# Loading the SwiGLU input weights first and multiplying them on VectorE, in a one-token attention and MLP kernel

## The chip, the cores and the metric

The kernel runs on one core of a Trainium2 chip. The metric is the device time of one execution in microseconds (us), the median of several executions. TensorE appears as PE (matmuls) and PEld (weight loads), VectorE as DVE, ScalarE as ACT, GpSimd as POOL and SyncE as SP.

## What is computed

One token `x` of 512 numbers is layer-normalised to `xn`, and two branches are added to it, all in float32:

```python
xn  = layernorm(x)
# attention over a cache: 32 heads, 4096 positions, 128 numbers a head
q   = (xn @ wq).reshape(32, 128)                       # wq 512 x 4096
s   = einsum("hd,hkd->hk", q, k_cache) * 128 ** -0.5   # k_cache 32 x 4096 x 128
o   = einsum("hk,hkd->hd", softmax(s), v_cache)
A   = o.reshape(4096) @ wo                             # wo 4096 x 512
# a gated MLP on the same token, weighted by its router score
g   = silu(xn @ w_gate); u = xn @ w_up                 # both 512 x 1376
y   = ((g * u) @ w_down) * sigmoid(xn @ w_r)           # w_down 1376 x 512
out = x + A + xn + y
```

With one token chosen out of one, the selection and the scatter of the original reference do nothing. The inputs are 159.45 MB, nearly all of it `k_cache` and `v_cache` (67.1 MB each), `wq` and `wo` (8.4 MB each) and the three MLP matrices (2.8 MB each).

## The kernel before

SBUF holds three large slots of 64 KB per partition: S0, S1 and S2. All large loads are issued by SP, in program order, one after another in one queue. Each goes to 128 partitions, except that `wo` is cut into seven pieces of 8, 8, 6, 5, 3, 1 and 1 rows per partition (`PIECES`).

The order of the queue is `wq` into S0; `k_cache` of groups 0 and 1 into S1 and S2; and then for each group g of four heads the values V[g] into S0 and the keys K[g+2] into the slot that group g's keys had. V[7] goes to S1. After the loop come `w_gate` and `w_up` (L76, both into S0), `w_down` (L246, into S2) and the pieces of `wo` (L251, into S1). A load into a slot waits, on SP, until the slot's earlier contents have been read, and everything behind it in SP's program waits with it.

The work runs in this order. VectorE normalises `x` and TensorE spreads it to `xb` (L163, L166), one column per partition. TensorE makes all queries in `ps_q` (L173), as soon as `wq` is there. For each group `scores(g)` multiplies the keys by the query on VectorE in place (L206), adds them up (L207), takes a maximum (L208 to L211), and ScalarE exponentiates (L214). `values(g)` multiplies probabilities and values on TensorE (L225, 32 matmuls of 512 columns, each issued as two instructions since it is float32), and gathers the head's own rows from the result (L230, L232).

After the loop TensorE turns the attention output into columns (`ot`, L273, L275); multiplies gate and up (`ffn_in`, L280), the 1376 hidden units lying along the free axis, 344 in each of four partition groups; VectorE and ScalarE make `hid`, and VectorE spreads it over partitions (four copies at L299, a transpose at L304, a masking at L306) to suit `w_down`, which was loaded as a flat run of 5504 numbers per partition; TensorE multiplies `w_down` in 43 matmuls (L312); ScalarE copies `y` (L315). Last, `add` (L324) sums everything into four accumulators of 128 columns: the residual first, then `y`, then 32 rows of `wo`, each as four matmuls. TensorE runs its instructions in program order, so no row of `wo` is multiplied before `y` is ready. Two copies on ScalarE and two on VectorE (L338, L340) and two stores (L341, L342) end the kernel.

Of the kernel before, what the change touches and what calls it, by code (L numbers as in the profile page):

```python
# [23 lines left out]
def kernel(  # L24
# [13 lines left out]
    nc = tc.nc  # L38
    _, H, Sk, Dh = k_cache.shape
    D = x.shape[-1]  # L40
    F = w_gate.shape[1]
    NK = D // P
    C = Sk // PP
    NG = H // HP
    DC = D // NCOL
    FC = F // NCOL
    FW = F * D // P
    NQ = FW // DC
    FA = F // PP
# [8 lines left out]
    def sb(name, shape, dt=F32):  # L58
        return const.tile(shape, dt, name=name)

    pad = sb("pad", [P, 96])
    S0, S1, S2 = (sb(f"slot{i}", [P, SLOT]) for i in range(3))


    KS = [S1, S2] * (NG // 2)
    VS = [S0] * (NG - 1) + [S1]

    loads = []

# [12 lines left out]
    x_row, xn = (t[0:1].rearrange("o c h -> o (c h)") for t in PT)  # L82
    xc = pv[0:1].rearrange("o c d -> o (c d)")
    loads.append(nc.scalar.dma_start(x_row, x[0]))
    wr_row = sb("wr_row", [1, D])
    loads.append(nc.scalar.dma_start(wr_row, w_r.rearrange("(o n) -> o n", o=1)))
    WQ = load_rows(wq, S0).rearrange("p (j g h d) -> p j g h d", j=NK, h=HP, d=Dh)
    K, V = {g: load_cache(k_cache, g, KS[g]) for g in range(2)}, {}


    ps_q = [psum.tile([P, 512], F32, name=f"ps_q{i}") for i in range(2)]
    ps_pv = [psum.tile([P, 512], F32, name=f"ps_pv{i}") for i in range(2)]
    ps_o = psum.tile([P, 512], F32, name="ps_o")
    ps_acc = psum.tile([P, 512], F32, name="ps_acc")
    ps_a = psum.tile([P, 512], F32, name="ps_a")
    ps_b = psum.tile([P, 512], F32, name="ps_b")
    for t in (ps_a, ps_b, ps_acc, *ps_pv):
        nc.vector.memset(t, 0.0)

    ones = sb("ones", [1, P])  # L100
    nc.vector.memset(ones, 1.0)
    eps_t = sb("eps_t", [1, 1])
    nc.vector.memset(eps_t, EPS)

    WIN = 2 * H - HP

    ints = sb("ints", [P, NQ * NCOL], I32)  # L110

    def hits(n, pattern, base, mult, mask):
        it = ints[:n]
        for _, k in pattern[::-1][:-1]:
            it = it.rearrange("p (a b) -> p a b", b=k)
        if len(pattern) == 1:
            it = it[:, :pattern[0][1]]
        else:
            it = it[:, :pattern[0][1], :]
        nc.gpsimd.iota(it, pattern=pattern, base=base, channel_multiplier=mult)  # L120
        if mask:
            nc.vector.tensor_scalar(it, it, mask, None, op0=ALU.bitwise_and)
        return it
# [3 lines left out]
    it = hits(P, [[-HP, G], [-1, HP]], 0, 1, 31)  # L127
# [6 lines left out]

    ew = sb("ew", [H, P + HP - 1])
    it = hits(H, [[1, P + HP - 1]], 1 - HP, -HP, 0)
    nc.vector.tensor_scalar(ew, it, 0, None, op0=ALU.is_equal)

    sy = sb("sy", [P, NCOL, PP])
    nc.gpsimd.memset(sy, 0.0)  # L140
    it = hits(P, [[-1, NCOL]], 0, 1, 31)
    nc.vector.tensor_scalar(sy[:, :, 0], it, 0, None, op0=ALU.is_equal)

    own = sb("own", [P, NQ, NCOL])
    it = hits(P, [[1, NQ], [-1, NCOL]], 0, 3, 3)
    nc.vector.tensor_scalar(own, it, 0, None, op0=ALU.is_equal)


    s1 = sb("s1", [1, 1])
    nc.vector.reduce_sum(s1, x_row, axis=AX.X)  # L150
    mean = sb("mean", [1, 1])
    nc.vector.tensor_scalar(mean, s1, 1.0 / D, None, op0=ALU.mult)
    nc.vector.tensor_scalar(xc, x_row, mean, None, op0=ALU.subtract)
    nc.vector.tensor_tensor(xn, xc, xc, op=ALU.mult)
    s2 = sb("s2", [1, 1])
    nc.vector.reduce_sum(s2, xn, axis=AX.X)
    std = sb("std", [1, 1])
    nc.scalar.activation(std, s2, AF.Sqrt, bias=eps_t, scale=1.0 / D)
    rstd = sb("rstd", [1, 1])
    nc.vector.reciprocal(rstd, std)  # L160
    nc.vector.tensor_scalar(xn, xc, rstd, None, op0=ALU.mult)  # L161
    for j in range(NK):
# [15 lines left out]
    nc.vector.tensor_tensor(wr_row, wr_row, xn, op=ALU.mult)  # L178
    r = sb("r", [1, 1])
    nc.vector.reduce_sum(r, wr_row, axis=AX.X)  # L180
    nc.tensor.matmul(ps_b[:, 0:1], ones, r, start=True, stop=True)  # L181
    base = wr_row
    nc.vector.tensor_tensor(base, x_row, xn, op=ALU.add)

    for t in PT:
        last_pool = nc.gpsimd.memset(t, 0.0)

    def sigmoid(z, e):
        nc.scalar.activation(e, z, AF.Exp, scale=-1.0)  # L189
        nc.vector.tensor_scalar(e, e, 1.0, None, op0=ALU.add)  # L190
        nc.vector.reciprocal(e, e)
        return e

    sr = sigmoid(ps_b[:, 0:1], sb("sr", [P, 1]))

    sc = [sb(f"sc{i}", [P, C]) for i in range(2)]
    rs = sb("rs", [P, NG])
    m = sb("m", [P, 1])
# [36 lines left out]
    for g in range(NG):  # L235
        scores(g)
        V[g] = load_cache(v_cache, g, VS[g])
        if g + 2 < NG:
            K[g + 2] = load_cache(k_cache, g + 2, KS[g + 2])
        values(g)  # L240


    W_GATE = load_rows(w_gate, S0[:, :FW]).rearrange("p (j f) -> p j f", f=F)
    W_UP = load_rows(w_up, S0[:, FW:2 * FW]).rearrange("p (j f) -> p j f", f=F)
    WD = S2[:, :FW].rearrange("p (j n) -> p j n", n=DC)
    loads.append(nc.sync.dma_start(S2[:, :FW], w_down.rearrange("f n -> (f n)").rearrange("(p j) -> p j", p=P)))  # L246
    WO = S1.rearrange("p (r n) -> p r n", n=D)
    src = wo.rearrange("(p r) n -> p r n", p=P)
    a = 0
# [6 lines left out]
    for i in (*loads, last_pool):  # L256
        tc.add_manual_dep(seen.ins, i.ins.name, mybir.DependencyInfo(mybir.DependencyClass.Sync, mybir.DependencyReason.DATA),
                          reason="seen before the store")
    at = [FW]

    def spare(n):
        at[0] += n
        return S2[:, at[0] - n:at[0]]

    rinv = sb("rinv", [H, 1])
# [4 lines left out]
    for c in range(HP):  # L272
        nc.tensor.matmul(ps_pv[0][:, :R], ew[:, HP - 1 - c:HP - 1 - c + P], o_n[:, c * R:(c + 1) * R],  # L273
                         start=(c == 0), stop=(c == HP - 1))
    nc.vector.tensor_copy(ot, ps_pv[0][:, :R])  # L275

    def ffn_in(W, ps):
        for j in range(NK):
            for t in range(NCOL):
                nc.tensor.matmul(ps[PP * t:PP * t + 1, :FC], xb[:, j, 0:1], W[:, j, t * FC:(t + 1) * FC],  # L280
                                 start=(j == 0), stop=(j == NK - 1), skip_group_check=True)
        return ps[:, :FC]

    gate = ffn_in(W_GATE, ps_a)
    hid = sigmoid(gate, spare(FC))
    nc.vector.scalar_tensor_tensor(hid, hid, sr, gate, op0=ALU.mult, op1=ALU.mult)
    up = ffn_in(W_UP, ps_b)
    nc.vector.tensor_tensor(hid, hid, up, op=ALU.mult)

    A8 = PP // 4
    XW = NQ + 9
    X = spare(XW * PP).rearrange("p (j a b) -> p j a b", a=A8, b=4)
    for b in range(4):
        first, rest = NQ * b // 4, NQ * b % 4
        n = (NQ - 1 + rest) // 4 + 1
        h = hid.rearrange("p (a i) -> p i a", i=FA)[:, first:first + n, :]
        nc.vector.tensor_copy(  # L299
            X[:, 3 - rest:3 - rest + 4 * n, :, b].rearrange("p (i s) a -> p i s a", s=4),  # L300
            h[:, :, None, :].to_broadcast([P, n, 4, A8]),
        )
    XT = spare(NQ * PP)
    nc.vector.transpose(XT, X[:, 3:3 + NQ].rearrange("p j a b -> p (j a b)"))  # L304
    hw = spare(NQ * NCOL).rearrange("p (j c) -> p j c", c=NCOL)
    nc.vector.tensor_tensor(hw, own, XT.rearrange("p (j k) -> p j k", k=PP)[:, :, 0:1].to_broadcast([P, NQ, NCOL]),  # L306
                            op=ALU.mult)
    ps_y = ps_pv[1]
    nc.vector.memset(ps_y, 0.0)  # L309
    for j in range(NQ):  # L310
        o = PP * (j % NCOL)
        nc.tensor.matmul(ps_y[o:o + NCOL, :DC], hw[:, j, :], WD[:, j, :], start=(j < NCOL),  # L312
                         stop=(j >= NQ - NCOL), skip_group_check=True)
    y = spare(DC)
    nc.scalar.activation(y, ps_y[:, :DC], AF.Copy)  # L315

# [3 lines left out]
    def add(w, rows, **flags):  # L322
        for c in ORDER:
            nc.tensor.matmul(acc[c], w(c), rows(c), skip_group_check=True, **flags)  # L324

    def quarter(t):
        return lambda c: t[:, c * DC:(c + 1) * DC]

    add(lambda c: ones[:, 0:1], quarter(base), start=True, stop=False)
    add(lambda c: sy[:, c, 0:1], lambda c: y, start=False, stop=False)  # L330
    for i in range(R):
        add(lambda c: ot[:, i:i + 1], quarter(WO[:, i, :]), start=False, stop=(i == R - 1))
    res = spare(D)[0:1].rearrange("o (h n) -> o h n", h=2)
    dst = out[0].rearrange("o (h n) -> o h n", h=2)
# [36 lines left out]
```

## Time and profile before

| | us |
|---|---|
| median of 3 runs | 377.63 (377.52 to 377.94) |
| the profiled execution | 377.58 |
| its span, first to last instruction | 375.8 |
| VectorE busy | 301.4 |
| TensorE busy (matmul) | 114.3 |
| ScalarE, GpSimd busy | 25.7, 3.2 |
| HBM read | 159.45 MB, 424 GB/s over the span |

Shares of busy time are of the span. A matmul's end is modelled, so a busy PE is not a PE at its peak. The profiled execution's time is 1.78 us more than its span.

### The profile page before, as it was taken

The page shows a single profiled execution, that of the slowest core. Times are in us where ns is not written, and L with a number is a line of the kernel's source. Part 1 is how long each engine was busy: PE and PEld are TensorE (multiplying, and loading weights), DVE is VectorE, ACT ScalarE, POOL GpSimd, SP SyncE. Part 2 cuts the span into 40 slices and gives each one's busy share as a digit, 9 for nine tenths or more (in the row PEclk, how much of TensorE's full clock was granted, in tenths as well). Part 3 has the DMA queues.
Part 4 walks back from the last instruction along what each step waited for, and adds up shares of the span by engine and source line. Part 5 has one row for each costly group of instructions (what it writes and reads, how often), then busy time and mean ns, then how long its engine had stood idle before and what let it go on. Part 6 is the DMA issues. An engine that isn't in the chain of part 4 may idle for free.

```text
span 375.8 us, 2511 instructions
## 1 busy us (share of the span) xinstructions
PE 114.3 (30%) x1096; PEld 40.9 (11%) x1096; DVE 301.4 (80%) x91; ACT 25.7 (7%) x80; POOL 3.2 (1%) x17
## 2 busy tenths in 40 slices
PE   0254000037001910091008100730064005458384
PEld 0211000012000200020001000110011001113163
DVE  6300599999999999999999999998999699910710
ACT  1100000020002002000200020002000200020000
POOL 2100000000000000000000000000000000000000
PEclk9998555559555775577557755595559556959879
DMA  8999998999999998999999998999999999999995
GB/s 335 446 446 446 446 446 363 419 446 441 446 446 446 446 413 377 446 446 433 446 447 434 446 426 384 446 447 433 439 448 432 439 432 398 439 416 427 427 424 218
DMA packets 3906, 159.60 MB, mean 425 GB/s; under 512 B 436, under 2 KB 438, under 8 KB 824
## 3 DMA queue, kind: packets, MB, share of 16 engines
q1 hardware_dynamic: 3890, 159.45, 98.5%
q8 instruction: 8, 0.13, 0.1%
q14 instruction: 2, 0.02, 0.0%
q10 hardware_dynamic: 6, 0.01, 0.0%
HBM read 159.45 MB, written 0.00 MB: 424 GB/s over the span
## 4 chain that ended last, share of the span: by engine, by line
DMA 80%; PE 19%; issue 0%; DVEq 0%; DVE 0%; SPq 0%
DMA slot<-in_A_v_cache_dram 60%; PE ps_pv L225 17%; DMA slot<-in_A_wo_dram 7%; DMA slot<-in_B_w_up_dram 7%; DMA slot<-in_A_wq_dram 6%; PE ps_q L173 2%; PE ps_q L324 0%; DVEq L366 0%; DVE slot L340 0%; PE ps_acc L324 0%; PE ps_b L181 0%; SPq L251 0%; PE ps_o L324 0%
## 5 line engine op out<-in xcount | busy, mean ns | idle before, releaser
L206 DVE TENSOR_TENSOR slot<-slot,ps_q 128x16384 f32<-128x16384 f32 x8 | 137.7, 17216 | 13.6 <-DMA slot<-in_A_k_cache_dram 13.6
L207 DVE TENSOR_REDUCE sc<-slot 128x128 f32<-128x16384 f32 x8 | 137.8, 17220 | 0.3
L225 PE MATMUL ps_pv<-slot,pt 128*16 128x512 f32 x512 | 73.4, 737 | 82.1 <-DMA slot<-in_A_v_cache_dram 82.1
L220 PE MATMUL ps_b<-rs,hselw 128*32 128x1 f32 x16 | 2.1, 200 | 140.0 <-ACT pt L214 140.0
L225 PEld LDWEIGHTS ps_pv<-slot,pt 128*16 128x16 f32 x512 | 16.2, 113 | 132.6 <-DMA slot<-in_A_v_cache_dram 75.0
L214 ACT ACTIVATE pt<-sc,nm 32x128 f32<-32x128 f32 x32 | 16.6, 518 | 130.4 <-DVE nm L211 130.0
L220 PEld LDWEIGHTS ps_b<-rs,hselw 128*32 128x32 f32 x16 | 1.4, 140 | 141.9 <-ACT pt L214 94.5
L230 ACT ACTIVATE pv<-ps_pv 128x512 f32<-128x512 f32 x8 | 4.8, 597 | 159.2 <-PE ps_pv L225 159.2
L190 DVE TENSOR_SCALAR sr<-sr 128x1 f32<-128x1 f32 x1 | 0.2, 155 | 18.0 <-ACT sr L189 18.0
L173 PE MATMUL ps_q<-slot,xb 128*32 128x512 f32 x64 | 9.4, 753 | 10.4 <-DMA slot<-in_A_wq_dram 10.4
L340 DVE COPY slot<-ps_o 1x128 f32<-1x128 f32 x1 | 0.3, 284 | 15.0 <-PE ps_acc L324 15.0
L232 PE MATMUL ps_o<-pv,selw 128*32 128x128 f32 x64 | 8.5, 276 | 6.3 <-ACT pv L230 6.3
L270 DVE TENSOR_SCALAR slot<-ps_o,rinv 32x128 f32<-32x128 f32 x1 | 0.3, 339 | 11.6 <-PE ps_o L232 11.6
L324 PE MATMUL ps_q<-slot,slot 128*1 128x128 f32 x128 | 7.9, 272 | 2.0 <-issue 1.3
L232 PEld LDWEIGHTS ps_o<-pv,selw 128*32 128x32 f32 x64 | 6.3, 109 | 13.6 <-ACT pv L230 13.6
L324 PE MATMUL ps_o<-slot,slot 128*1 128x128 f32 x64 | 7.8, 272 | 0.0
L324 PE MATMUL ps_acc<-slot,slot 128*1 128x128 f32 x64 | 7.6, 272 | 0.0
L312 PE MATMUL ps_pv<-slot 128*4 128x128 f32 x86 | 4.4, 388 | 7.2 <-DVE ps_pv L309 7.2
L324 PEld LDWEIGHTS ps_q<-slot,slot 128*1 128x1 f32 x128 | 6.1, 83 | 3.3 <-issue 1.6
L214 ACT ACTIVATION_READ_ACCUMULATOR pt<-sc,nm 32x1 f32 x32 | 6.3, 198 | 0.0
L163 PE MATMUL ps_a<-ones,pt 1*128 1x32 f32 x8 | 2.1, 417 | 10.2 <-DVE pt L161 10.2
L324 PEld LDWEIGHTS ps_acc<-slot,slot 128*1 128x1 f32 x64 | 5.1, 83 | 0.0
(79 smaller groups left out, 58.2 us busy)
## 6 DMA issues: line engine op xcount, KB each, us to landing
slot<-in_A_wo_dram SPq DMA_DIRECT2D x2, 2048.0 KB, 23.4
slot<-in_B_w_gate_dram SPq DMA_DIRECT2D x1, 2752.0 KB, 21.5
slot<-in_B_w_up_dram SPq DMA_DIRECT2D x1, 2752.0 KB, 25.4
slot<-in_B_w_down_dram SPq DMA_DIRECT2D x1, 2752.0 KB
slot<-in_A_wo_dram SPq DMA_DIRECT2D x1, 1536.0 KB
slot<-in_A_wo_dram SPq DMA_DIRECT2D x1, 1280.0 KB, 27.6
slot<-in_A_wo_dram SPq DMA_DIRECT2D x1, 768.0 KB
slot<-in_A_wo_dram SPq DMA_DIRECT2D x2, 256.0 KB, 27.3
```

Source lines behind the costliest of these rows:

```text
L163: nc.tensor.matmul(ps_a[:, j * PP:(j + 1) * PP], xn.rearrange("o (p j) -> o j p", j=NK)[:, j, :], ones[:, :PP], start=True, stop=True)
L173: nc.tensor.matmul(ps_q[i][h * PP:(h + 1) * PP, :], xb[:, j, :], WQ[:, j, i * GH:(i + 1) * GH, h, :], start=(j == 0), stop=(j == NK - 1), ...
L206: nc.vector.tensor_tensor(k, k, q[:, None, :].to_broadcast([P, C, Dh]), op=ALU.mult)
L207: nc.vector.tensor_reduce(s, k, axis=AX.X, op=ALU.add)
L214: nc.scalar.activation(PT[g % 2][o, :, h], s[o, :], AF.Exp, bias=nm[o, :], scale=SCALE, accum_out=rs[o, g:g + 1])
L220: nc.tensor.matmul(ps_b[:H, 0:1], hselw[:, w], rs[:, g:g + 1], start=(g == 0), stop=(g == NG - 1), skip_group_check=True)
L225: nc.tensor.matmul(ps[o:o + G * HP, :], p[:, G * i:G * (i + 1), :].rearrange("p c h -> p (c h)"), v[:, G * i:G * (i + 1), :].rearrange("p ...
L230: nc.scalar.activation(pv.rearrange("p c d -> p (c d)"), ps, AF.Copy)
L232: nc.tensor.matmul(ps_o[:H, :Dh], selw[:, c, w], pv[:, c, :], start=(g == 0 and c == 0), stop=(g == NG - 1 and c == G - 1), skip_group_che ...
L270: nc.vector.tensor_scalar(o_n, ps_o[:H, :Dh], rinv, None, op0=ALU.mult)
L312: nc.tensor.matmul(ps_y[o:o + NCOL, :DC], hw[:, j, :], WD[:, j, :], start=(j < NCOL), stop=(j >= NQ - NCOL), skip_group_check=True)
L324: nc.tensor.matmul(acc[c], w(c), rows(c), skip_group_check=True, **flags)
```

## The change

`w_gate` and `w_up` move from the end of the load queue to its head. `w_gate` goes into S2, on partitions 32 to 95 only, eight rows of the matrix per partition, as four loads of 16 partitions that lie four apart. `w_up` follows into S1, then `wq` into S0 as before, and the loads of K[0] and K[1] are issued behind the new gate and up work. The two key slots swap (K[0] in S2), so V[7] goes to S2.

Gate and up are no longer matmuls with a moving weight matrix. VectorE multiplies each of the eight (gate) or four (up) weight rows per partition by that partition's number of normalised `x` and adds them up into one row of 1376 sums; TensorE then only adds these over the partitions, against a column of ones, in 16 matmuls each, so that the hidden units come out spread over partitions: ten per partition for units 0 to 1279, six more on every fourth of partitions 32 to 95 for the last 96. `x` for the gate (`xg`) is loaded once more, eight numbers per partition, and normalised there with the mean and 1/std that a small matmul broadcasts. GpSimd clears the partitions that the loads leave empty. `hid` is finished before the first scores.

`w_down` goes into S0 after V[6], as ten whole rows of 512 per partition and a second load of 16 partitions with six rows each, behind a GpSimd clear. Its product is 16 matmuls of 512 columns instead of 43 of 128. The copies, the transpose, the mask and the two constants they needed (`own`, `sy`) are gone. In the diff PP is 32, GP 64, GJ 8, FR 10, XR 6 and NX 16.

```diff
-    KS = [S1, S2] * (NG // 2)
-    VS = [S0] * (NG - 1) + [S1]
+    KS = [S2, S1] * (NG // 2)
+    VS = [S0] * (NG - 1) + [S2]
...
+    xg = sb("xg", [P, GJ])
+    nc.gpsimd.memset(xg, 0.0)
+    loads.append(nc.scalar.dma_start(xg[PP:PP + GP], x[0, 0].rearrange("(p j) -> p j", j=GJ)))
...
+    W_GATE = S2[:, :GJ * F].rearrange("p (j f) -> p j f", f=F)
+    src, dst = (t.rearrange("(a b) f -> a b f", b=4)
+                for t in (w_gate.rearrange("(p j) f -> p (j f)", j=GJ), S2[PP:PP + GP, :GJ * F]))
+    for b in range(4):
+        loads.append(nc.sync.dma_start(dst[:, b], src[:, b]))
+    W_UP = load_rows(w_up, S1[:, :FW]).rearrange("p (j f) -> p j f", f=F)
     WQ = load_rows(wq, S0).rearrange("p (j g h d) -> p j g h d", j=NK, h=HP, d=Dh)
-    K, V = {g: load_cache(k_cache, g, KS[g]) for g in range(2)}, {}
...
+    nc.tensor.matmul(ps_b[:, 2:4], ones, stat, start=True, stop=True)
+    mr = sb("mr", [P, 2])
+    nc.vector.tensor_copy(mr, ps_b[:, 2:4])
+    nc.vector.tensor_scalar(xg, xg, mr[:, 0:1], mr[:, 1:2], op0=ALU.subtract, op1=ALU.mult)
+    shares = [S1[:, FW + i * F:FW + (i + 1) * F] for i in range(2)]
+    for j in range(GJ):
+        nc.gpsimd.memset(W_GATE[:PP, j, :], 0.0)
+    nc.gpsimd.memset(shares[0][PP + GP:], 0.0)
...
+    def ffn_in(t, W, xcol, rows, ps):
+        for j in range(W.shape[1]):
+            if j == 0:
+                nc.vector.tensor_scalar(t[:rows], W[:rows, j, :], xcol(j)[:rows], None, op0=ALU.mult)
+            else:
+                nc.vector.scalar_tensor_tensor(t[:rows], W[:rows, j, :], xcol(j)[:rows], t[:rows], op0=ALU.mult, op1=ALU.add)
+        for r in range(FR):
+            nc.tensor.matmul(ps[:, r:r + 1], t[:, :FR * P].rearrange("p (m r) -> p r m", r=FR)[:, r, :], onec,
+                             start=True, stop=True)
+        cols = wide.rearrange("p (s g c) -> p s g c", s=XR, c=4)
+        nc.vector.tensor_copy(cols, t[:, x0:F].rearrange("p (g s) -> p s g", s=XR)[:, :, :, None]
+                              .to_broadcast([P, XR, 3 * PP // 4, 4]))
+        for i in range(XR):
+            nc.tensor.matmul(ps[:3 * PP, FR + i:FR + i + 1], wide[:, 3 * PP * i:3 * PP * (i + 1)], onec,
+                             start=True, stop=True)
+        return ps[:, :NX]
+
+    gate = ffn_in(shares[0], W_GATE, lambda j: xg[:, j:j + 1], PP + GP, ps_a)
+    up = ffn_in(shares[1], W_UP, lambda j: xb[:, j, 0:1], P, ps_b)
+
+    K, V = {g: load_cache(k_cache, g, KS[g]) for g in range(2)}, {}
...
+    hid = sigmoid(gate, sb("hid", [P, NX]))
+    nc.vector.scalar_tensor_tensor(hid, hid, sr, gate, op0=ALU.mult, op1=ALU.mult)
+    nc.vector.tensor_tensor(hid, hid, up, op=ALU.mult)
...
-    W_GATE = load_rows(w_gate, S0[:, :FW]).rearrange("p (j f) -> p j f", f=F)
-    W_UP = load_rows(w_up, S0[:, FW:2 * FW]).rearrange("p (j f) -> p j f", f=F)
-    WD = S2[:, :FW].rearrange("p (j n) -> p j n", n=DC)
-    loads.append(nc.sync.dma_start(S2[:, :FW], w_down.rearrange("f n -> (f n)").rearrange("(p j) -> p j", p=P)))
+    WD = S0[:, :FR * D].rearrange("p (r n) -> p r n", n=D)
+    loads.append(nc.sync.dma_start(WD, w_down[:FR * P].rearrange("(p r) n -> p r n", r=FR)))
+    WX = S0[:, FR * D:NX * D].rearrange("p (r n) -> p r n", n=D)
+    last_pool = nc.gpsimd.memset(WX[:3 * PP], 0.0)
+    loads.append(nc.sync.dma_start(WX[PP:PP + GP].rearrange("(a b) r n -> a b r n", b=4)[:, 0],
+                                   w_down[FR * P:].rearrange("(a r) n -> a r n", r=XR)))
...
-    for j in range(NQ):
-        o = PP * (j % NCOL)
-        nc.tensor.matmul(ps_y[o:o + NCOL, :DC], hw[:, j, :], WD[:, j, :], start=(j < NCOL),
-                         stop=(j >= NQ - NCOL), skip_group_check=True)
-    y = spare(DC)
-    nc.scalar.activation(y, ps_y[:, :DC], AF.Copy)
+    for i in range(NX):
+        o = PP * (i % NCOL)
+        k = slice(0, P if i < FR else 3 * PP)
+        nc.tensor.matmul(ps_y[o:o + 1, :], hid[k, i:i + 1], (WD[k, i, :] if i < FR else WX[k, i - FR, :]),
+                         start=(i < NCOL), stop=(i >= NX - NCOL), skip_group_check=True)
+    y = spare(D)
+    nc.scalar.activation(y, ps_y, AF.Copy)
...
-    add(lambda c: sy[:, c, 0:1], lambda c: y, start=False, stop=False)
+    add(lambda c: onec, quarter(y), start=False, stop=False)
```

## Rows read from the trace of the kernel before

**Rows 1.** The page: the span, and part 1, busy time and instructions of each engine.

```profile
span 375.8 us, 2511 instructions
PE 114.3 (30%) x1096; PEld 40.9 (11%) x1096; DVE 301.4 (80%) x91; ACT 25.7 (7%) x80; POOL 3.2 (1%) x17
```

**Rows 2.** The chain of work that ended last, in order of time: start, length, what.

```profile
0.73 21.79 DMA slot<-in_A_wq_dram
22.66 9.39 PE ps_q L173 x64
...
321.21 25.44 DMA slot<-in_B_w_up_dram
...
346.71 25.93 DMA slot<-in_A_wo_dram
...
372.69 0.27 PE ps_q L324
```

**Rows 3.** Busy time of the engines in stretches between landings: the stretch, its length, busy us (instructions) of PE, PEld, DVE, ACT and POOL, the granted TensorE clock, the busy share of the DMA engines, and GB/s.

```profile
81.00:121.05 40.05, 10.48 (x74) 3.10 (x74) 39.80 (x7) 2.68 (x9) 0.00 (x0) 0.63 0.97 419
121.05:159.67 38.62, 10.94 (x74) 3.25 (x74) 38.37 (x7) 2.69 (x9) 0.00 (x0) 0.63 1.00 435
...
275.50:314.17 38.67, 10.56 (x74) 2.92 (x74) 35.28 (x7) 2.66 (x9) 0.00 (x0) 0.63 1.00 434
...
333.50:346.65 13.15, 11.80 (x88) 4.18 (x92) 0.53 (x2) 0.60 (x1) 0.00 (x0) 0.83 1.00 427
346.65:372.60 25.95, 16.70 (x410) 10.79 (x402) 8.49 (x11) 0.73 (x2) 0.00 (x0) 0.87 0.95 403
```

**Rows 4.** DMA queues (packets, MB, share of 16 engines' span) and issues by line (size, median us from issue to landing).

```profile
q8 instruction: 8, 0.13, 0.1%
...
slot<-in_B_w_gate_dram SPq DMA_DIRECT2D x1, 2752.0 KB, 21.5
```

**Rows 5.** The timeline, the first half: when SP issues a load, and what VectorE does at its two edges.

```profile
0.73 0.39 SPq L76 DMA_DIRECT2D slot<-in_A_wq_dram  x1
...
12.33 0.29 DVE L166 COPY xb<-ps_a 128x128 f32<-128x128 f32 x1 [2.16 <-PE ps_a L163]
...
41.91 17.22 DVE L206 TENSOR_TENSOR slot<-slot,ps_q 128x16384 f32<-128x16384 f32 x1 [8.96 <-DMA slot<-in_A_k_cache_dram]
...
76.42 0.33 SPq L72 DMA_DIRECT2D slot<-in_A_k_cache_dram  x1
```

**Rows 6.** Instructions grouped by line, operation and shape: count, busy us, mean ns of one, idle time before them.

```profile
L206 DVE TENSOR_TENSOR slot<-slot,ps_q 128x16384 f32<-128x16384 f32 x8 | 137.7, 17216 | 13.6 <-DMA slot<-in_A_k_cache_dram 13.6
...
L230 ACT ACTIVATE pv<-ps_pv 128x512 f32<-128x512 f32 x8 | 4.8, 597 | 159.2 <-PE ps_pv L225 159.2
...
L163 PE MATMUL ps_a<-ones,pt 1*128 1x32 f32 x8 | 2.1, 417 | 10.2 <-DVE pt L161 10.2
...
L186 POOL MEMSET pt<- 128x512 f32 x2 | 1.0, 530 | 8.8 <-DVE wr_row L183 8.8
...
L299 DVE COPY slot<-slot 128x352 f32<-128x352 f32 x2 | 1.6, 791 | 0.0
...
L286 DVE SCALAR_TENSOR_TENSOR slot<-slot,sr,ps_a 128x344 f32<-128x344 f32 x1 | 0.6, 575 | 0.1
```

**Rows 7.** The timeline of the end: start, length, engine, line, operation, and in brackets idle time of the engine before it with its releaser.

```profile
318.65 0.33 SPq L76 DMA_DIRECT2D slot<-in_B_w_gate_dram  x1
...
329.40 0.29 DVE L208 TENSOR_REDUCE m<-sc 128x1 f32<-128x128 f32 x1
...
333.59 9.22 PE L225 MATMUL ps_pv<-slot,pt 128*16 128x512 f32 x64 [0.67 <-DMA slot<-in_A_v_cache_dram]
334.40 0.19 PEld L225 LDWEIGHTS ps_pv<-slot,pt 128*16 128x16 f32 x4 [0.66 <-issue]
335.25 0.19 PEld L225 LDWEIGHTS ps_pv<-slot,pt 128*16 128x16 f32 x4 [0.66 <-issue]
...
340.05 0.12 PEld L225 LDWEIGHTS ps_pv<-slot,pt 128*16 128x16 f32 x4 [0.31 <-issue]
340.48 0.12 PEld L225 LDWEIGHTS ps_pv<-slot,pt 128*16 128x16 f32 x4 [0.31 <-issue]
...
346.31 0.19 DVE L275 COPY slot<-ps_pv 128x32 f32<-128x32 f32 x1 [1.24 <-PE ps_pv L273]
...
357.65 0.48 DVE L309 MEMSET ps_pv<- 128x512 f32 x1
...
362.94 0.27 PE L324 MATMUL ps_q<-slot,sy 128*1 128x128 f32 x1
...
368.81 0.27 PE L324 MATMUL ps_q<-slot,slot 128*1 128x128 f32 x1 [1.34 <-issue]
...
371.46 0.27 PE L324 MATMUL ps_q<-slot,slot 128*1 128x128 f32 x1 [0.52 <-DMA slot<-in_A_wo_dram]
...
372.69 0.27 PE L324 MATMUL ps_q<-slot,slot 128*1 128x128 f32 x1 [0.17 <-DMA slot<-in_A_wo_dram]
...
373.78 0.32 SPq L342 DMA_DIRECT2D out_dram<-slot  x1
```

**Rows 8.** Two stretches of the end, in the columns of rows 3: the matmuls of `w_down`, and the first rows of `wo`.

```profile
358.20:362.50 4.30, 4.30 (x90) 2.92 (x94) 0.00 (x0) 0.00 (x0) 0.00 (x0) 0.57 0.99 424
362.90:367.20 4.30, 4.26 (x155) 4.03 (x156) 0.00 (x0) 0.00 (x0) 0.00 (x0) 1.00 1.01 426
```

More of the change, by code (lines that the diff above doesn't have):

```diff
@@ L45 @@
     DC = D // NCOL
-    FC = F // NCOL
     FW = F * D // P
-    NQ = FW // DC
-    FA = F // PP
+    GP = P // 2
+    GJ = D // GP
+    FR = F // P
+    XR = (F - FR * P) // 16
+    NX = FR + XR
     R = H * Dh // P
@@ L96 @@
     ps_b = psum.tile([P, 512], F32, name="ps_b")
-    for t in (ps_a, ps_b, ps_acc, *ps_pv):
+    for t in (ps_a, ps_b, *ps_pv):
         nc.vector.memset(t, 0.0)
@@ L101 @@
     nc.vector.memset(ones, 1.0)
+    onec = sb("onec", [P, 1])
+    nc.vector.memset(onec, 1.0)
     eps_t = sb("eps_t", [1, 1])
@@ L108 @@
     WIN = 2 * H - HP
-    ints = sb("ints", [P, NQ * NCOL], I32)
+    ints = sb("ints", [P, P + HP - 1], I32)
     def hits(n, pattern, base, mult, mask):
-        it = ints[:n]
+        total = 1
+        for _, k in pattern:
+            total *= k
+        it = ints[:n, :total]
         for _, k in pattern[::-1][:-1]:
             it = it.rearrange("p (a b) -> p a b", b=k)
[L116 to L119, printed above, removed]
         nc.gpsimd.iota(it, pattern=pattern, base=base, channel_multiplier=mult)
@@ L137 @@
     nc.vector.tensor_scalar(ew, it, 0, None, op0=ALU.is_equal)
[L139 to L146, printed above, removed]
     s1 = sb("s1", [1, 1])
     nc.vector.reduce_sum(s1, x_row, axis=AX.X)
-    mean = sb("mean", [1, 1])
+    stat = sb("stat", [1, 2])
+    mean, rstd = stat[:, 0:1], stat[:, 1:2]
     nc.vector.tensor_scalar(mean, s1, 1.0 / D, None, op0=ALU.mult)
@@ L158 @@
     nc.scalar.activation(std, s2, AF.Sqrt, bias=eps_t, scale=1.0 / D)
-    rstd = sb("rstd", [1, 1])
     nc.vector.reciprocal(rstd, std)
@@ L166 @@
     nc.vector.tensor_copy(xb.rearrange("p j n -> p (j n)"), ps_a[:, :NK * PP])
+    nc.tensor.matmul(ps_b[:, 2:4], ones, stat, start=True, stop=True)
[6 more added lines that the diff above has]
+    nc.gpsimd.memset(shares[0][PP + GP:], 0.0)
+    wide = S1[:, FW + 2 * F:FW + 2 * F + 3 * PP * XR]
+    x0 = FR * P - XR * PP // 4
+    def ffn_in(t, W, xcol, rows, ps):
[17 more added lines that the diff above has]
+    K, V = {g: load_cache(k_cache, g, KS[g]) for g in range(2)}, {}
     GH = NG // 2
@@ L180 @@
     nc.vector.reduce_sum(r, wr_row, axis=AX.X)
-    nc.tensor.matmul(ps_b[:, 0:1], ones, r, start=True, stop=True)
+    ps_r = ps_pv[0][:, 0:1]
+    nc.tensor.matmul(ps_r, ones, r, start=True, stop=True)
     base = wr_row
@@ L185 @@
     for t in PT:
-        last_pool = nc.gpsimd.memset(t, 0.0)
+        nc.gpsimd.memset(t, 0.0)
     def sigmoid(z, e):
@@ L192, in sigmoid @@
         return e
-    sr = sigmoid(ps_b[:, 0:1], sb("sr", [P, 1]))
+    sr = sigmoid(ps_r, sb("sr", [P, 1]))
+    nc.vector.memset(ps_r, 0.0)
+    hid = sigmoid(gate, sb("hid", [P, NX]))
+    nc.vector.scalar_tensor_tensor(hid, hid, sr, gate, op0=ALU.mult, op1=ALU.mult)
+    nc.vector.tensor_tensor(hid, hid, up, op=ALU.mult)
     sc = [sb(f"sc{i}", [P, C]) for i in range(2)]
@@ L258 @@
                           reason="seen before the store")
-    at = [FW]
+    at = [NX * D]
     def spare(n):
         at[0] += n
-        return S2[:, at[0] - n:at[0]]
+        return S0[:, at[0] - n:at[0]]
     rinv = sb("rinv", [H, 1])
@@ L275 @@
     nc.vector.tensor_copy(ot, ps_pv[0][:, :R])
[L277 to L307, printed above, removed]
     ps_y = ps_pv[1]
     nc.vector.memset(ps_y, 0.0)
-    for j in range(NQ):
-        o = PP * (j % NCOL)
-        nc.tensor.matmul(ps_y[o:o + NCOL, :DC], hw[:, j, :], WD[:, j, :], start=(j < NCOL),
-                         stop=(j >= NQ - NCOL), skip_group_check=True)
-    y = spare(DC)
-    nc.scalar.activation(y, ps_y[:, :DC], AF.Copy)
+    for i in range(NX):
[5 more added lines that the diff above has]
+    nc.scalar.activation(y, ps_y, AF.Copy)
     acc = [t[c * PP:c * PP + 1, :DC] for c, t in enumerate((*ps_q, ps_o, ps_acc))]
```

## The prediction

> **What bounds the kernel now.** The first view is the page's busy time [rows 1]: VectorE looks like the bound with 80% of the span, but no engine is full. The second is the chain of waits [rows 2]: it is transfers nearly from end to end, `wq` from 0.73 us, then the values, then `w_gate`/`w_up`, then `wo`, whose last piece releases the last matmul at 372.69 us. The third is the table of stretches [rows 3]: from the second group on every period of one K and one V load takes 38.62 to 38.67 us with the DMA share at 1.00 and 434 to 435 GB/s. VectorE is busy 38.4 of these at first and 35.3 in the last, so it follows the transfers. The MLP matrices at the end run at 427 GB/s, also at share 1.00. So what sets the time is the stream of 159 MB, plus about 1 us between SP's first issue and its first bytes, plus what follows the last landing: one row of `wo`, two copies and a store. A change gains only if it shortens the stream or one of these two ends, and loses only if it lets the queue run dry or makes something finish after the last landing.
>
> **The bytes.** The change moves `w_gate` and `w_up` from the end to the front and loads as many bytes as before. The stretch that held them is 13.15 us [rows 3]; everything from `wq` to V[7] therefore shifts by about +13.15 us, and `w_down` plus `wo` follow V[7] directly. Sum over the stream: 0.
>
> **More loads in the queue.** There are four `w_gate` loads instead of one and two of `w_down` instead of one: +4. How much one boundary costs is bounded by comparing stretches: a period of two loads moves 16.78 MB at 435 GB/s, the stretch of two smaller loads runs at 427 [rows 3]. Put wholly on the boundaries, the deficit of 13.15 × (1 − 427/435) = 0.24 us is 0.1 us for each, so 4 × 0.1 = 0.4 us above; below it is 0. I take +0.2 us. The second load of `x` is 2 KB and goes to ScalarE's queue: 0.
>
> **The start.** `wq`'s first issue takes 0.39 us on SP for 128 rows [rows 5]; the first load is now 16 rows. Its issue cannot take less than nothing, so the gain is 0 to 0.39 us; loads issued later have fully hidden issue times. I take −0.1 us.
>
> **The new work at the front.** It has to be out of two slots in time. `wq` landed at 22.5 us and will land at 35.7, and K[0] needs S2 by then; K[1] needs S1 19.4 us later (K[0] took 22.5 to 41.9 [rows 2, 5]), at 55. On VectorE, the spread `x` was ready at 12.6 us [rows 5], and `w_gate` will have landed by about 3.1 + 6.6 = 9.7 us (the stream's first bytes at 22.5 − 19.4, half of 13.15 behind them). A fused multiply-add over 1376 numbers costs between 1.05 ns a number (17,216 ns for 16,384) and 1.67 (575 for 344) [rows 6]: 1.45 to 2.30 us. Eight of them are 11.6 to 18.4 us, so S2 is read by 24 to 31, and K[0] is issued 5 to 11 us before its turn. GpSimd's clears of 1376 take 530 × 1376/512 = 1.42 us each, eight in 11.4 us, beside it, starting before. Up adds 5.8 to 9.2 us and the two spreading copies of 576 numbers 1.3 us each (791 for 352): 33 to 43 us. The 16 matmuls of up are 32 instructions; at the 0.26 us that line 163 took (2.1 us for eight) 8.4 us. S1 is free by 41 to 51, before 55. The queries wait behind this on TensorE: 9.39 us from 41 to 51 on, so 51 to 61, where K[0] lands at 55.1. Late queries would delay the scores of group 0, and with them SP's issue of K[2], by up to 6 us; it was issued at 76.42, 4.6 us before V[0] landed at about 81.0 [rows 2, 3, 5]. I take the lower half, no delay. Everything here is covered by 25 us of `wq` and K[0] transfers; uncovered it would cost 20 us and more.
>
> **The middle.** Slots swap but the waits stay: V[g+1] behind V[g]'s matmuls, K[g+2] behind VectorE. At the end `w_down` waits for V[6]'s matmuls, as `w_gate` did at 318.65 [rows 7] (+13.15 = 332); its second load waits for a clear of 3072 numbers on GpSimd, 3.2 us. `wo` now waits for VectorE's last scores, over by 329.40 + 13.15 = 342.6 [rows 7]. SP's queue must be fed again by 346.7, when V[7] has landed. All are in time: 0.
>
> **The end of TensorE's program.** Here the change takes away cover. V[7]'s matmuls began at 333.59, 39 us before the last `wo` row; now they begin at 333.59 + 13.15 = 346.74, 26 us before it. What follows is in order: `ot` was finished 12.91 us later (346.31 + 0.19 − 333.59), so at 359.65. A clear of `ps_y`, 0.48: 360.14. The new 32 instructions of 512 columns run in eight groups of four; a group of four of line 225 took 0.43 us at clock 1.00 and 0.85 earlier in the same stage [rows 7]. At 0.43: 3.44 us, to 363.6. Some 0.2 us to drain, the copy of 512 numbers 0.60 [rows 6], `y`'s own matmuls 0.22: the rows of `wo` begin at R = 364.6. Before, `y`'s began at 362.94 and the rows at about 363.2. Gone are 5 us of gate and up matmuls, the chain of `hid` and its spreading, yet R is 1.4 us later.
>
> From R, 32 rows at 0.222 us (155 matmuls in 4.30 us, eight a row [rows 8]) need 7.1 us, to 371.7. That alone stays ahead of the last landing. But one row of the trace shows more: at 368.81 a matmul within a row had waited 1.34 us for "issue", for nothing that the profile shows, while the waits for `wo` come later, at 371.46 and 372.69 [rows 7]. The page lists 8 instruction transfers [rows 4] for TensorE's 2192 instructions [rows 1], so blocks of about 274, or 17 rows of `wo`; I read this stall as TensorE having used up its program. If a block is asked for when the one before is entered, that was 17 rows (3.8 us of work) before 367.4, at 363.6, and it came 5.2 us later. With such a delay the last row is issued at R + 15 rows + 5.2 = R + 8.5 us, wherever the border lies: before, 371.7, hidden under the landing at 372.69; now 373.1, 0.4 us after it. Bounds of this term: 0 (a block that arrives 0.5 us sooner) and, with the delay 0.3 us longer, +0.7. I take +0.2.
>
> The Trainium skill (Runtime: NRT & Kernel Launch, Instruction fetch mechanics) says that crossing a 16 KiB block of instructions costs little and is mostly hidden; by that this term would be 0 and the sum 377.7. The 1.34 us row disagrees as I read it.
>
> **The sum**, against the profiled execution's 377.58 us (span 375.8 plus 1.78 around it, and 0.05 below the median): −0.1 + 0.2 + 0.2 = +0.3, so 377.9 us. A measurement of this kernel tells 0.2%, 0.76 us, from no change; 377.9 lies within it.
>
> **The rivals.**
>
> *TensorE's tail takes over (slower).* The rows decide as soon as R + 8.5 passes 372.7, R = 364.2; my R is already 0.4 beyond. If the eight groups of `w_down` run at the slower 0.85 us, as the clock of 0.57 in the same place before shows is possible [rows 8], R is 368.0 and the last row 376.5: +3.8 us, 381.4. With a block 1 us later it is 378.9. Against it: TensorE idled for over 7 us before that stage, and now goes on from V[7] with gaps of about a microsecond. The likelier form is a part of this: 378.4 to 380. Chance 0.17.
>
> *The four loads do not run into one another (slower).* A load alone takes up to 2.0 us for 1 KB (store issued at 373.78, span over at 375.8 [rows 1, 7]); four more such, 8 us: 385.6. The last stretch, seven `wo` pieces and `w_down` with a DMA share of 0.95 including its run-out, speaks against it. Chance 0.05. The Trainium skill (SBUF — State Buffer, Summary: rules for kernel authors) asks for 128 partitions and one DMA, not several, where transfers bound the kernel; by that page's 2 us plus bytes at 436 GB/s, an estimate, four loads of 0.70 MB would take 14.5 us in place of 8.5 for one of 2.82 MB, and the sum would be 383.9; no run here shows it yet.
>
> *The new work at the front holds the queue (slower).* Late by 6 us at the queries, K[2] is issued 1.4 us after the queue has run dry: 379.3. Chance 0.05.
>
> *The stream itself shrinks (faster).* The first full period took 40.05 us against 38.62 [rows 3], 1.43 us that nothing in these rows explains. If it belonged to how the first loads lined up and the new order loses it, and the start gives its 0.39, the time is 375.8 to 376.8. It decides from a gain of 0.8 us, more than half of the deficit. Chance 0.13.
>
> **How the numbers follow.** The forecast has 0.60. Faster by over 0.2% has 0.13, slower 0.17 + 0.05 + 0.05 = 0.27. The range runs from 377.1 (half of the first period's loss, about 0.1 of the chance below it) to 379.2, which takes in the tail's smaller forms and leaves the slow clock and the separate loads out, some 0.1.
>
> **What would show it.** Right: V[7]'s matmuls begin near 346.7, `wo`'s rows near 364.6, periods stay at 38.6 us, K[0] is issued by 31 us and the DMA share has no gap near 36 or 55 us; the last matmul waits for `wo` or for issue within a microsecond of 373. Wrong: a share below 1.00 in the first 36 us, SP waiting for VectorE when `wq` has landed, a granted clock of 0.5 between 360 and 372, or a shorter second period.

## The result, and the profile after

The changed kernel takes 380.16 us (median of 6, 379.48 to 380.77) against 377.57 for the kernel before: 1.0067 times as long, 95% interval 1.0053 to 1.0081, so 2.5 us slower. The forecast was no change, 377.9, with 379.2 as the upper end. In the experiments below one execution of b_late2_split (694.0 us) and one of the kernel before (425.82 us) lie far outside, and the ratios leave both out.

The profiled execution took 380.39 us, its span 378.6. The page's busy times, to be held against [rows 1]:

```profile
span 378.6 us, 2441 instructions
PE 124.3 (33%) x1044; PEld 50.8 (13%) x1044; DVE 315.3 (83%) x98; ACT 25.7 (7%) x80; POOL 17.0 (5%) x25
```

VectorE has 13.9 us more work; none of it shows in the time by itself: it lies in the first 34 us, under the loads of `w_up`, `wq` and K[0]. The stretches between landings of values, in the columns of [rows 3]:

```profile
95.48:135.64 40.16, 10.92 (x74) 3.22 (x75) 39.91 (x7) 2.69 (x9) 0.00 (x0) 0.63 1.01 434
135.64:174.32 38.68, 11.32 (x74) 3.23 (x74) 38.43 (x7) 2.68 (x9) 0.00 (x0) 0.63 1.00 434
...
290.17:328.77 38.60, 10.85 (x75) 2.94 (x75) 35.32 (x7) 2.66 (x9) 0.00 (x0) 0.63 1.00 435
328.77:349.13 20.36, 10.33 (x74) 2.89 (x75) 16.14 (x6) 2.66 (x9) 2.66 (x1) 0.75 0.96 415
```

The periods are as long as before to 0.1 us; only the last stretch, up to V[7]'s matmuls, is longer, 20.36 us against 19.37 (314.22 to 333.59). But V[0]'s matmuls begin at 95.48, 14.33 us later than before (81.15) instead of 13.15, and V[7]'s at 349.13, 15.54 us later than the 333.59 of [rows 7]: 2.39 us beyond the shift by the moved bytes. That is nearly the whole loss, and it has come in before the tail begins. The timeline at the places that matter:

```profile
26.97 13.53 SPq L74 DMA_DIRECT2D slot<-in_A_k_cache_dram  x2
...
56.86 17.22 DVE L251 TENSOR_TENSOR slot<-slot,ps_q 128x16384 f32<-128x16384 f32 x1 [4.94 <-DMA slot<-in_A_k_cache_dram]
...
91.36 0.33 SPq L74 DMA_DIRECT2D slot<-in_A_k_cache_dram  x1
...
362.48 5.31 PE L328 MATMUL ps_pv<-slot,hid 128*1 128x512 f32 x32 [0.94 <-DVE ps_pv L324]
...
375.95 0.28 DVE L356 COPY slot<-ps_o 1x128 f32<-1x128 f32 x1 [13.53 <-PE ps_acc L340]
```

K[0] is issued at 26.97, in good time, but VectorE gets it at 56.86 instead of the forecast 55.1, so K[2] is issued at 91.36. At the end `w_down`'s 32 instructions take 5.31 us, not 3.44. From the chain of waits: `y`'s sum begins at 368.50 and the rows of `wo` run to the end without waiting for a load, where before the last one did [rows 2]:

```profile
368.50 0.27 PE ps_q L340
368.80 0.09 PE ps_q L340
...
375.78 0.09 PE ps_q L340
375.97 0.27 DVE slot L356
```

Two theories come out of this. **M**: K[2]'s load was issued so shortly before the queue ran dry that it started slowly. A load of 8.4 MB is split over 16 DMA engines, each of which moves eight packets of 64 KB here, and the trace's packet records tell when each engine is done. The first was done with V[0] at 93.25, 1.89 us after K[2]'s issue (3.90 us in the kernel before), and the first packets of K[2] took up to 3.9 us, where 2.42 is usual; on the mean of the 16 engines K[2] took 1.1 us longer, unevenly spread. **T**: the tail on TensorE, the forecast's first rival. A third, **start**, blames the first loads. At V[7] the engines' mean is 1.1 us later than the kernel before's plus 13.15 us (346.30 against 332.05) and the slowest engine 2.2 us (348.55 against 333.16): half of the lateness is in all of them, half in their spread. The longer last stretch is in the spread: a block of instructions (queue q8) was loaded under V[7] at 332.64, and the engine that carried it was done at 348.55, the other 15 by 347.75.

### The profile page after: what moved, and what is told of

Read it like the earlier page. It is cut to its first block, busy times and chain, and to the rows that moved or that the text cites. A ratio compares the mean times of both kernels' runs of the same rounds, so it can differ in the third digit from the quotient of the medians.

```text
span 378.6 us, 2441 instructions
## 1 busy us (share of the span) xinstructions
PE 124.3 (33%) x1044; PEld 50.8 (13%) x1044; DVE 315.3 (83%) x98; ACT 25.7 (7%) x80; POOL 17.0 (5%) x25
## 4 chain that ended last, share of the span: by engine, by line
DVE 61%; DMA 29%; PE 7%; issue 1%; ACT 0%; DVEq 0%; ACTq 0%
DVE sc L252 27%; DVE slot L251 27%; DMA slot<-in_A_k_cache_dram 18%; DMA slot<-in_A_v_cache_dram 12%; DVE slot L191 3%; PE ps_pv L270 2%; PE ps_q L340 2%; PE ps_pv L328 1%; PE ps_a L167 1%; DVE slot L189 0%; DVE pv L158 0%; DVE ew L150 0%; DVE m L253 0%; PE ps_pv L319 0%; PE ps_o L277 0%
## 5 line engine op out<-in xcount | busy, mean ns | idle before, releaser
L291 POOL MEMSET slot<- 96x3072 f32 x1 | 2.7, 2658 | 297.2 <-PE ps_pv L270 297.2
L191 DVE SCALAR_TENSOR_TENSOR slot<-slot,xg,slot 96x1376 f32<-96x1376 f32 x7 | 11.5, 1646 | 0.7
L181 POOL MEMSET slot<- 32x1376 f32 x8 | 10.2, 1316 | 0.0
L193 PE MATMUL ps_a<-onec,slot 128*128 128x1 f32 x20 | 4.7, 364 | 15.4 <-DVE slot L191 15.4
L193 PEld LDWEIGHTS ps_a<-onec,slot 128*128 128x128 f32 x20 | 4.6, 320 | 15.5 <-issue 15.5
```

The costliest lines, as they stand in the source:

```text
L181: nc.gpsimd.memset(W_GATE[:PP, j, :], 0.0)
L191: nc.vector.scalar_tensor_tensor(t[:rows], W[:rows, j, :], xcol(j)[:rows], t[:rows], op0=ALU.mult, op1=ALU.add)
L193: nc.tensor.matmul(ps[:, r:r + 1], t[:, :FR * P].rearrange("p (m r) -> p r m", r=FR)[:, r, :], onec, start=True, stop=True)
```

## The experiments

Times are medians; each ratio is to executions of the kernel before taken beside it (median 377.33 to 377.44), with its 95% interval in brackets.

**a_yearly**: `w_down`'s matmuls move into `values(7)`, behind V[7]'s.

```diff
+        if g == NG - 1:
+            for i in range(NX):
+                nc.tensor.matmul(ps_y[o:o + 1, :], hid[k, i:i + 1], ...)
         nc.scalar.activation(pv.rearrange("p c d -> p (c d)"), ps, AF.Copy)
```

> The changed kernel, with the 16 matmuls of w_down moved ahead of the regrouping of the attention output on TensorE (right behind V[7]'s matmuls, into the free accumulator ps_a, cleared at the front), and the loads of w_down and wo issued before values(7). In the changed kernel y was ready at 368.5 and the last row of wo was multiplied at about 375.9, while the last landing by the trace is near 375.0. Theory T (the tail on TensorE sets the end): y is ready 3 to 4 us sooner, the rows of wo wait for their loads again, and the time falls by about 0.5 to 0.9 us, to 379.3 to 379.7. Were the tail the whole of the loss, it would fall by 2.6 us, to 377.6. Theory S (the stream of transfers itself ends 2.3 us later): not below 379.2.

379.41 us (377.82 to 380.4), 1.0052 [1.0034, 1.0069]. The median is as T expects; the interval overlaps that of the changed kernel, so this run alone doesn't show a gain. One execution took 377.82, the one profiled: there K[2] started almost normally (0.2 us an engine lost) and V[7]'s matmuls began at 346.90. So T alone is small, and something else varies between executions by some 2 us.

**a_onegate**: one load for `w_gate`.

```diff
-    for b in range(4):
-        loads.append(nc.sync.dma_start(dst[:, b], src[:, b]))
+    loads.append(nc.sync.dma_start(S2[PP:PP + GP, :GJ * F], w_gate.rearrange("(p j) f -> p (j f)", j=GJ)))
```

> The changed kernel with w_gate as one load of 64 partitions instead of four of 16. Theory S, part start: the first loads cost 0.5 us more than their bytes, and if that comes from the four separate loads and their four issues on SP (2.68 us together), one load gives back 0.3 to 0.5 us, to 379.7 to 379.9. If the 0.5 us come with any first load, no change (380.2). If four loads were the good way to start, slower by 0.3 us or more.

379.86 us, 1.0063 [1.0051, 1.0075]: no difference that can be told. The number of `w_gate` loads is not it.

**a_short0**: 2.15 us less of VectorE's work in group 0.

```diff
+        n = C - 8 if g == 0 else C
...
-        nc.vector.tensor_tensor(k, k, ...)
-        nc.vector.tensor_reduce(s, k, ...)
+        nc.vector.tensor_tensor(k[:, :n], k[:, :n], ...)
+        nc.vector.tensor_reduce(s[:, :n], k[:, :n], ...)
```

> The changed kernel with VectorE's scores of group 0 made 2.15 us shorter: only 120 of the 128 positions per partition are multiplied and added up, the scores of the other eight are left out (set to 0). SP then issues K[2] about 4 us before V[0]'s last bytes instead of 1.9 us. Theory M (a load issued too shortly before the queue runs dry starts slowly and sets some DMA engines back for good): faster by 0.7 to 1.5 us, to 378.7 to 379.5, and the first full period is below 39.4 us. Theory T, and start alone: no change, 380.2.

378.68 us, 1.0035 [1.0024, 1.0046]: half of the loss is gone. The values' first and last matmuls:

```profile
95.32 8.38 PE L273 MATMUL ps_pv<-slot,pt 128*16 128x512 f32 x64 [2.75 <-DMA slot<-in_A_v_cache_dram]
133.93 9.55 PE L273 MATMUL ps_pv<-slot,pt 128*16 128x512 f32 x64 [5.90 <-DMA slot<-in_A_v_cache_dram]
...
346.59 5.61 PE L273 MATMUL ps_pv<-slot,pt 128*16 128x512 f32 x32 [0.72 <-DMA slot<-in_A_v_cache_dram]
```

V[0] is as late as in the changed kernel, but the first period is 38.61 us instead of 40.16, and V[7] lands for 346.59, 0.15 us before the forecast 346.74. What is left (1.3 us over the kernel before) lies behind V[7]: `w_down`'s matmuls take 5.31 us, as in the changed kernel, and one wait comes back:

```profile
PE ps_acc L343 <- issue: 1.2, 1, 1.2
```

TensorE waits inside a row of `wo` for "issue" again. Counted in the trace, this wait and that of [rows 7] stand behind the same instruction of TensorE's program, the 1984th recorded, here and in the kernel before, a_onegate and b_late2 (and, at 0.7 to 1.4 us, in a_split, a_nofetch, b_split and b_pe48), though the programs differ.

**b_late2, b_late1**: the kernel before with 2.0 or 1.0 us of extra VectorE work in group 0 (a reciprocal of 300 or 150 numbers per partition).

```diff
+        if g == 0:
+            nc.vector.reciprocal(dly, dly)
         nc.vector.tensor_reduce(s, k, axis=AX.X, op=ALU.add)
```

> The kernel before with an extra VectorE instruction of 2.0 us (a reciprocal on a scratch tile) between the two large instructions of group 0, so that K[2] is issued 2.0 us later, at 78.4, with about 1.9 us of V[0] left to land, as in the changed kernel. Theory M: slower by 0.7 to 1.5 us, to 378.3 to 379.1. Theory T, and start alone: no change, 377.6, since VectorE catches up by group 5.

> b_late2 with half the extra work (1.0 us): K[2] is issued at about 77.4, with about 2.9 us of V[0] left to land. Theory M: between the two, 377.4 to 378.4, with single executions at either end if the effect has an edge there.

b_late2: 378.68 us, 1.0039 [1.0027, 1.0051]. b_late1: 377.51 us, 1.0007 [0.9996, 1.0017]; nine executions lie at or below 377.83 and two at 378.90 and 379.08. A loss of the kind can be made in the kernel before by 2 us of VectorE work, although VectorE has time to spare later (from the seventh group on it waits for keys again, as before); 1 us is near the edge.

**b_late2_split, b_split, a_split**: scores of group 0 and the load of K[2] in two halves.

```diff
+        n = C // 2 if g == 0 else C
+        for a in range(0, C, n):
+            kh = k[:, a:a + n]
+            nc.vector.tensor_tensor(kh, kh, ...)
+            nc.vector.tensor_reduce(s[:, a:a + n], kh, ...)
...
+        n = SLOT // 2 if cache is k_cache and g == 2 else SLOT
+        for a in range(0, SLOT, n):
+            loads.append(nc.sync.dma_start(t[:, a:a + n], src[:, a:a + n]))
```

> b_late2 (2.0 us of extra VectorE work in group 0 of the kernel before), with group 0's scores made in two halves and K[2] loaded in the same two halves, the extra work standing in the second half. VectorE is as late as in b_late2, but the queue has half of K[2] some 20 us ahead. Theory M (it is the load that is issued too shortly before the queue runs dry): back to the kernel before, 377.2 to 377.8. If VectorE's lateness itself cost the 1.3 us, 378.7 as b_late2.

> The kernel before with K[2] and group 0's scores in halves and nothing else. Theory M: K[2] was issued 3.9 us ahead and paid nothing, so no change, 377.2 to 377.6; if even there something is lost, up to 0.7 us faster and the best of all versions.

> The changed kernel with K[2] in halves, w_down's matmuls left where they are. Theory M plus T: as a_short0, 378.4 to 379.0 (the tail's clock and the wait for code remain), 0.6 to 1.0 us above a_split_early; if the halves alone cure everything, 377.8.

b_late2_split: 377.32 us, 0.9998 [0.9989, 1.0007]. By the edit VectorE is as late as in b_late2 (no trace of a 377 us execution was kept to show it), and the loss is gone: it was the load's late issue. b_split: 377.37, 0.9999 [0.999, 1.0008], nothing to gain where K[2] came in time. a_split: 379.07 (378.18 to 379.49), 1.0042 [1.003, 1.0055], a little above the range expected: M cured (V[7]'s matmuls begin at 346.66), T left. Its fastest execution, the profiled one, ran `w_down`'s matmuls at full clock (granted 1.00, 3.62 us):

```profile
360.39 3.62 PE L334 MATMUL ps_pv<-slot,hid 128*1 128x512 f32 x32 [0.94 <-DVE ps_pv L330]
```

**a_split_early, a_best**: a_split with a_yearly's edit; a_best with a_onegate's besides.

> The changed kernel with both cures that keep the result: group 0's scores are made in two halves of 64 positions per partition and K[2] is loaded in the same two halves, so that its first half is issued about 17 us sooner, at 74 us; and the matmuls of w_down stand right behind V[7]'s as in a_yearly. Theory M plus T (the slow start of K[2]'s load and the tail on TensorE make up the whole loss, the stream being otherwise as predicted): V[7]'s matmuls begin at 346.6, wo's rows wait for their loads, and the time is that of the kernel before within 0.4 us, 377.0 to 377.8. If the first loads cost something of their own, 378 to 378.7.

> a_split_early with w_gate as one load of 64 partitions. Theory M plus T: no difference from a_split_early, 377.0 to 377.8. If the four first loads cost 0.3 to 0.5 us, that much faster than a_split_early.

a_split_early: 377.86 us (377.50 to 378.48), 1.0014 [1.0006, 1.0023]. a_best: 378.17, 1.0022 [1.0013, 1.0031], so one load is no better here either. In a_split_early K[2]'s first half is issued at 74.26, V[7]'s matmuls begin at 346.94, and the rows of `wo` wait for their loads as in the kernel before:

```profile
74.26 17.64 SPq L77 DMA_DIRECT2D slot<-in_A_k_cache_dram  x2
```

```profile
PE ps_q L346 <- DMA slot<-in_A_wo_dram: 2.6, 4, 1.6
```

M and T together are 2.0 of the 2.5 us (1.0067 to 1.0014).

**a_nofetch, b_pe48**: why K[0] came late. By the DMA table of 36 to 56 us, K[0]'s stretch, the changed kernel loads a block of instructions there (queue q8):

```profile
q1 hardware_dynamic: 142, 8.32, 96.2%
q8 instruction: 1, 0.02, 0.3%
```

The first part of this diff is a_nofetch's (which also leaves 26 sums out of `ffn_in`), the second b_pe48's, ahead of the queries:

```diff
         values(g)
+        if g == 0:
+            for i in range(2 * FR + XR):
+                nc.tensor.matmul(ps_a[:, 64 + i:65 + i], ident, onec, start=True, stop=True)
...
+    for i in range(12):
+        nc.tensor.matmul(ps_a[:, 256 + i:257 + i], ones, ones[:, 0:1], start=True, stop=True)
```

> The changed kernel with 26 of the 32 partition sums of gate and up left out on TensorE before the first scores (so the MLP's product is not the reference's) and 26 matmuls of the same shape put behind group 0's values, so that the count of instructions later is the same. TensorE then issues some 176 instead of 280 instructions before K[0] lands, fewer than one block of 256 with its first border near 192. Theory C (the load of a code block, at 42.8 us in the changed kernel, set back one DMA engine in the middle of K[0] and so made K[0], the first scores and K[2]'s issue 1.4 us late): the first scores start at about 55.5 instead of 56.9, K[2] is issued at about 90, and the time falls by 0.7 to 1.3 us, to 378.7 to 379.4. If K[0] is late by the first loads alone, the scores start at 56.9 as before and the time stays at 380.

> The kernel before with 12 tiny matmuls more (48 instructions) ahead of the queries, so that TensorE's first block border falls near 31 us, within K[0]'s load, instead of 84 us. Theory C: K[0] lands for VectorE at about 43.3 instead of 41.9, K[2] is issued at about 77.8 with 2.5 us left, and the time rises by 0.3 to 1.3 us, to 377.7 to 378.7. Otherwise 377.4.

a_nofetch: 379.32 us, 1.0048 [1.0036, 1.006], an interval that overlaps the changed kernel's; K[0] is ready 0.64 us sooner, and no instruction transfer lies in that stretch:

```profile
56.22 17.22 DVE L251 TENSOR_TENSOR slot<-slot,ps_q 128x16384 f32<-128x16384 f32 x1 [8.91 <-DMA slot<-in_A_k_cache_dram]
```

b_pe48: 378.86 us (377.38 to 379.54), 1.0028 [1.0013, 1.0043]:

```profile
43.50 17.22 DVE L208 TENSOR_TENSOR slot<-slot,ps_q 128x16384 f32<-128x16384 f32 x1 [9.87 <-DMA slot<-in_A_k_cache_dram]
```

Twelve matmuls that do nothing make the kernel before 1.1 to 2.2 us slower in six of eight executions, since K[0] is ready at 43.50 instead of the 41.91 of [rows 5]. The packet records show how. The block takes one of the 16 engines for 0.9 to 1.0 us, the packet behind it takes 2.9 us instead of 2.42, and that engine, 1.4 us behind by then, is the last to finish the load:

```
                   block at, us   packet behind it   its engine done   the other 15 by
before, K[2]        85.43  0.96         2.89             101.33             99.97
changed, K[0]       42.82  0.92         2.92              56.31             55.28
b_pe48, K[0]        34.32  0.96         2.89              42.98             41.70
```

So in the changed kernel the block is 1.0 of the 1.6 us by which the last bytes of K[0] (56.31) come later than in the kernel before (41.52) plus 13.15. The other 0.6 are there when `wq` has landed (35.97 against 22.20 plus 13.15), so they come with the first loads; why stays open. The number of `w_gate` loads is at most 0.3 of them (K[0] was ready at 56.54 in a_best, 56.83 in a_split_early).

The time between K[2]'s issue and the first engine's end of V[0], and what K[2] then took beyond its usual 19.32 us on the mean of the engines, both by the packet records of the profiled executions, against the time of all executions over the kernel before (the ratio times 377.4):

```
             us ahead   K[2] longer   loss, us
a_short0       4.13        0.0        1.3 (the tail's part)
before         3.90        0.1        0
a_nofetch      2.47        0.4        1.8 (with the tail's part)
b_late1        2.36        0.1        0.3, two executions of eleven 1.5
a_onegate      2.01        1.0        2.4 (with the tail's part)
a_yearly       1.92        0.2        2.0; the profiled execution 0.4
changed        1.89        1.1        2.5 (with the tail's part)
b_pe48         1.78        0.6        1.1, two executions of eight 0
b_late2        1.55        0.8        1.5
```

The margin alone does not decide: at 1.92 and 1.89 us K[2] lost 0.2 and 1.1. What else does, no run shows.

## Why the prediction was wrong

*Bytes, more loads, the start.* Right in size: with M cured, V[7]'s matmuls begin at 346.59 to 346.94 in a_short0, a_split and a_split_early, against 346.74. In part that is luck: when `wq` has landed, the engines are on average 0.2 to 0.5 us later than the kernel before's plus 13.15, where the start was to gain 0.1, and by V[0] this is made good (93.58 in a_short0, 93.62 forecast so) for no reason that was looked into. Four loads or one made no difference. The Trainium skill's rule for one load of 128 partitions (SBUF — State Buffer, Summary: rules for kernel authors), by which the time would have been 383.9, finds no support in this kernel: with `w_gate` in one load (of 64 partitions) a_onegate took 379.86, with four 380.16.

*The new work at the front.* The costs were right: a fused multiply-add took 1646 ns (1450 to 2300 forecast), S2 was free at 26.97 (24 to 31), the queries were ready by 50, a little before the range (51 to 61). **The step that failed is the end of this part**: "4.6 us before V[0] landed", "no delay". Two things were wrong in it. K[0] itself was expected on time: it was ready 1.8 us late, not through the queries but through its own transfer, in part behind a block of code, and so K[2] was late. And the margin was misread: 4.6 us counts to V[0]'s matmuls, while the first engine was done 3.90 us after the issue, and the price was set to begin where the queue is dry, in the third rival ("K[2] is issued 1.4 us after the queue has run dry: 379.3"). It begins some 2 us earlier: all of b_late2's 1.5 us are paid though K[2] was issued 1.55 us before the first engine was done with V[0]. A rival at 0.05 with the right place, the wrong threshold and another cause (late queries) was about half of the result: 0.9 us from the changed kernel to a_split, 1.2 to a_short0, 1.4 from a_yearly to a_split_early.

*The end of TensorE's program.* The mechanism, the first rival's, was right and one term was mis-sized. R was forecast at 364.6; in a_split, with `w_down`'s matmuls at full clock, `y`'s sum begins at 364.72 and so R is 364.9. But in the traces of the changed kernel, a_onegate, a_short0 and a_nofetch the eight groups took 5.31 us; here the changed kernel's, the stretch ahead of them and their own:

```profile
349.10:362.40 13.30, 11.20 (x80) 3.90 (x80) 0.99 (x3) 0.60 (x1) 0.00 (x0) 0.85 1.00 429
362.40:367.90 5.50, 5.42 (x40) 1.08 (x40) 0.02 (x1) 0.04 (x1) 0.00 (x0) 0.69 0.99 417
```

The granted clock fell to a mean of 0.69 of 2.4 GHz, that is to 1.2 GHz for most of the stretch, after 13 us in which TensorE had gaps of 0.4 to 0.9 us: 5.31 us instead of the 3.44 taken. I had argued that gaps of a microsecond would not do that; why the clock stayed full in a_split behind the same gaps is open. After it the wait for code behind the 1984th instruction came back, as forecast, in a_short0 (1.2 us); in the profiled execution of the changed kernel the code was there in time. The tail is worth 1.1 us (a_split to a_split_early). How a like loss is shared differs between traces: in a_onegate V[7]'s matmuls begin at 347.60, only 0.9 us after the forecast, and the tail, with 5.31 us and a wait of 1.2, adds the rest of 379.96. The Trainium skill's statement that a block border is mostly hidden (Runtime: NRT & Kernel Launch, Instruction fetch mechanics) holds for most borders here; at the end the rows show up to 1.4 us, and within K[0] the block costs the transfer, not TensorE.

*"The stream itself shrinks".* The first period's 1.43 us that nothing explained stands in the changed kernel too (40.16), for another reason: there it is K[2]'s slow start, and a_short0 without it has 38.61. In the kernel before it is the first block of code, loaded at 85.43 inside K[2]'s load: its engine was done 1.4 us behind the other 15 (the table of blocks above). So it was not how the first loads lined up.

Sum: M and T are 2.0 us together, and the share of each depends on which is cured first: M 0.9 to 1.4, T 0.6 (a_yearly, not clear of noise) to 1.1 (a_split to a_split_early). The last 0.5, which a_split_early still has over the kernel before, has no cause shown; the forecast had 0.3 for the first loads, the boundaries and the wait for code. No version beat the kernel before.

## What to carry to other kernels

In a kernel bound by its transfers, write down for each load how long before the queue's end it is issued, and treat a margin that shrinks below the two or three microseconds found here as a cost, not as slack; cut the load and the work that frees its buffer in halves to get it back. When a change moves work from one end of such a kernel to the other, check what now stands between the last large landing and the end, engine by engine, at the lower clock as well. And a few added instructions can move a code block's load under a critical transfer.

## What the runs showed of the hardware

- An 8.4 MB load issued 1.6 to 2.0 us before the first DMA engine ran out of the load ahead of it made the kernel 0.9 to 1.5 us slower (the changed kernel against a_split, b_late2), though one execution at 1.9 us hardly paid (a_yearly); at 2.4 us two executions of eleven paid (b_late1), at 3.9 us none did (the kernel before).
- A 16 KB block of instructions loaded under an 8.4 MB transfer set one of its 16 DMA engines back by 1.4 us, and the transfer landed 0.6 (a_nofetch against the changed kernel) to 1.6 us later (b_pe48): it is as late as its slowest engine.
- The granted clock of one stretch of 5 us was full in one execution (a_split, 3.62 us) and mostly half in another (the changed kernel, 5.31 us), with the same instructions ahead of it.
